# A new order of opening steps, a second two-bank PSUM buffer in blocks 1 and 2, and new turns for side work in a fused attention and two-MLP kernel

## The chip, the cores and the metric

One core of one Trainium2 chip runs the whole program in one launch. The metric is the device time of one execution in microseconds, the median of the runs. Engines are called PE (TensorE), DVE (VectorE), ACT (ScalarE), POOL (GpSimd) and SP (SyncE, which here only issues DMAs).

## The reference

Three stages follow each other; tokens are 8 batches x 576 positions = 4608, the model width is 512.

```python
# 1: attention inside chunks of 64 positions, 8 heads of 64
scores = scale * q_c @ k_c.T;  p = exp(scores - max);  out = (p / (p.sum() + 1e-9)) @ v_c
x = out.transpose(0, 2, 1, 3).reshape(4608, 512)
# 2: gated MLP, w_gate and w_val 512 x 1536, w_out 1536 x 512
xn = x / sqrt(mean(x * x) + 1e-6) * rms_g
g = xn @ w_gate;  y = (g * sigmoid(g) * (xn @ w_val)) @ w_out
# 3: second MLP, w_in 512 x 2048, w_out 2048 x 512, rational activation
h = y @ w_in
P = a0 + a1*h + a2*h*h + a3*h*h*h;  Q = 1 + |b0|*|h| + |b1|*h*h
out = (P / (Q + 1e-6)) @ w_out
```

Everything is float32.

## The kernel before

**Numbers in two parts.** A float32 operand is split into a high part (a cast on ACT) and a low part (value minus high part, usually on DVE), and each product runs as three matmuls, high by high, high by low, low by high (PASSES). Weights arrive as 64-bit words; `words_to_whole` joins the two words of each number: L121 and L126 on ACT, L128 and L131 on DVE. `split` then makes the high part on ACT (L135) and the low part (L137) on DVE, or on POOL where the weight unit's name stands in `ON_POOL`. The low part of an activation tile is made at L390, also on POOL where the tile's name (`x0`, ...) is in `ON_POOL`.

**Tokens.** There are 36 tiles of 128 tokens, four to a block, nine blocks. A tile's attention is a *visit*: `products` (L284) computes on PE into a two-bank PSUM tile `xs` the weighted values of tile x and the scores of tile x+1; DVE normalises (L322) and takes the maximum and subtracts it (L299, L301), ACT takes the exponential p (L308) and the sum of squares (L331), POOL a power (L333, L334), ACT scales xa by it (L475). `transposes` (L351 for p, L354 for xa) writes a second two-bank tile `tp`; ACT copies one half out as pT (L358), DVE multiplies the other by the gain into xf (L383), from which high and low parts go to the block's operand xT (L388, L390) or, in later blocks, to `rawx` and `right`. `xs` and `tp` share one pool tag, "at".

**The first MLP.** Blocks 0 to 2 are *plain*: `cell(j, f)` runs a gate product g and a value product v of 12 matmuls of 512 columns each (L495), with tanh on ACT (L504), L505 and L521 on DVE and a DMA of u to DRAM. A block has 12 cells. Blocks 3 to 8 go in three pairs: `group` computes the same by a scheme with seven products per 2 x 2 blocks (L532, tiles sa and sb, additions L564 and L552 on DVE), whose left operands `combos` and right operands `right_sums` prepare.

**Turns.** After the opening everything is counted in *turns*, a turn being one call of a cell half (12 matmuls) or one step of a group (6 or 12). `plan` maps a turn to side work: `VISIT_AT` is the turn of each visit and `BEHIND` how many turns later its transposes come; `UNIT_AT`, `COMBOS_AT`, `LEFT_AT`, `RIGHT_AT`, `STAGE_AT`, `WO_AT` place weight units, left sums, loads, right sums, staging of the second MLP's weights through DRAM, and the output weights. Blocks 0, 1 and 2 take turns 0 to 23, 24 to 47 and 48 to 71, the pairs turns 72 to 251.

**The output product** of the first MLP starts at turn 252: 90 items of `item_products` (L1039; accumulators a for block 0, then oa and ob). Each item needs a high part (L872) and a low part (L879) of u on ACT and DVE, some need a sum (L864). `left_sums` (L823, L827, L836 on DVE) prepares left operands, `stage` the second MLP's output weights at the turns in `QUAD_AT`. The **second MLP** follows (L1068, L1087).

**Order.** The opening up to the third cell of block 0 is written out by hand: `START` is a string whose letters each advance one generator by a step: 0 to 4 are the first five tiles, a to d the four quarters of weight unit 0, e and f the halves of unit 1, g unit 2, h to j the loads of later units, M, N and O the first three cells, and w one transpose of the identity into an unused bank, which keeps PE occupied. On the engines under `manual_schedule` instructions stay in program order; on the others a scheduler places them, by its own model of waits. All engines are manual in the opening, in plain(0) only SP, in blocks 1 and 2 ACT and DVE, later ACT.

**PSUM.** It has eight banks. `bank` gives single ones (tag "pp"), `two_banks` pairs (tag "at"). `stage_now` picks the counts: 3 singles and 2 pairs in the opening (beside the bank of the idle transposes), 6 and 1 from there to the last group, 4 and 2 in the end.

Of the kernel before, what the change touches and what calls it, by code (L numbers as in the profile page):

```python
# [9 lines left out]
F32 = mybir.dt.float32  # L10
# [13 lines left out]
NPL = 3  # L24
NSTART = 3
START = (
    "120c31wwwwwwwwwwwwwwwwwwwww03020wwww1a0wwwwww20101b4ce020cd21wwwwwww0020wwwwww30gf112131wwww"
    "1c32c0www033c1130132002123aawwwww32www131awww423213024a3wwwwwwwwwwwwww241a2w3bba3b2b343wwwww"
    "wwwMbdec24ddMdMbd4M4eMge4MfeNNdMegfgeiNfNMMgONhfOgfOOggjgNONOgOggg"
)  # L30
ON_POOL = ('w10.0', 'w10.1', 'w10.3', 'w11.0', 'w12.0', 'w12.2', 'x0', 'x1', 'x2', 'x4')
VISIT_AT = (8, 12, 16, 20, 25, 29, 33, 37, 49, 52, 55, 58, 61, 64, 67, 70, 73, 79, 85, 91, 97, 103, 109, 115, 133, 139, 145, 151, 157, 163, 169, 175,)
BEHIND = (4, 4, 4, 4, 4, 4, 4, 4, 2, 2, 2, 2, 2, 2, 2, 2, 4, 4, 4, 4, 4, 4, 4, 4, 4, 4, 4, 4, 4, 4, 4, 4,)
UNIT_AT = (6, 10, 14)
LEFT_AT = (62, 66, 70)
COMBOS_AT = (25, 31, 38, 45, 51, 58)
RIGHT_AT = (73, 120, 180)
STAGE_AT = (28, 74, 102, 134, 152, 171, 194, 222)
STAGE_FROM = (32, 78, 106, 138, 156, 175, 198, 226)
STAGE_EACH = (2, 1, 1, 1, 1, 1, 1, 1)  # L40
WO_AT = (196, 210, 224)
WO_FROM = (204, 218, 232)
OPEN_AT = 246
START_AT = (250, 251)
QUAD_AT = (262, 266, 270, 274, 278, 282, 286, 290, 294, 299, 303, 307, 311, 315, 319, 323)
LEFT_SUMS_AT = (255, 258, 261)
EARLY = 3
BLOCK0 = (
    (-20, "fetch", 0), (-18, "ring", 0), (-17, "split", 0, "B11"), (-16, "split", 0, "B21"), (-15, "sum", 0, "T1"),
# [7 lines left out]
def fused_kernel(  # L57
# [207 lines left out]
    ps_pool = [None]  # L265
    stage_now = [0]

    def bank(name):
        return ps_pool[0].tile([P, W], F32, tag="pp", bufs=(3, 6, 4)[stage_now[0]], name=name)

    def two_banks(shape, name):
        return ps_pool[0].tile(list(shape), F32, tag="at", bufs=(2, 1, 2)[stage_now[0]], name=name)

    def products(x, s):
        ps = two_banks([P, 2, 2, NP, CH], f"xs{x.i if x else ''}_{s.i if s else ''}")
# [62 lines left out]
    def transposes(x, p):  # L338
# [21 lines left out]
        if x:  # L360
# [329 lines left out]
    with ExitStack() as phase:  # L690
# [55 lines left out]

        opening.close()
        ps1 = ExitStack()
        ps_pool[0] = ps1.enter_context(tc.tile_pool(name="ps1", bufs=1, space=PSUM, reuse_waits="tile"))
        stage_now[0] = 1  # L750

        for u in range(3, NG):
            spread(UNIT_AT[u - 3], more[u], 1, 4, 4)
        for n, (turn, behind) in enumerate(zip(VISIT_AT, BEHIND)):
            visit(turn, TB + n, behind)
        spread(RIGHT_AT[0], right_sums(0), 1, 2, 5)
        for t in range(1, NSB):
            spread(RIGHT_AT[t], right_sums(t), 1, 1, 9)
        for g in range(NG):
            spread(COMBOS_AT[g], combos(g), 1, 2, 9)  # L760
        for u in range(3):
            at_turn(LEFT_AT[u], load_left, 0, u)
        for g in range(NF2 // 2):
            steps = stage_left(g)
            at_turn(STAGE_AT[g], next, steps)
            spread(STAGE_FROM[g], steps, 1, STAGE_EACH[g], 24 // STAGE_EACH[g])
        for u in range(3):
            steps = two_halves("wo", u, outs[u])
            at_turn(WO_AT[u], next, steps)
            spread(WO_FROM[u], steps, 1)  # L770

# [14 lines left out]
        with tc.manual_schedule(engines={mybir.EngineType.SP}):  # L786
            plain(0)
        with tc.manual_schedule(engines={mybir.EngineType.Activation, mybir.EngineType.DVE}):
            for j in range(1, NPL):
                plain(j)  # L790
        with tc.manual_schedule(engines={mybir.EngineType.Activation}):
# [146 lines left out]

            at_turn(OPEN_AT, open_o)
            for i in range(2):  # L940
                at_turn(START_AT[i], start_o, i)

            for t in range(NSB):
                running = {}
                used = 0
                for q, k in ORDER:
                    do(TURN[0])
                    if k == 0:
                        running[q] = group(t, q)
# [313 lines left out]
```

## Time and profile before

| | us |
|---|---|
| runs | 1691.86, 1694.39, 1694.63 |
| median | 1694.39 |
| profiled execution, its own time | 1692.62 |
| its span | 1690.8 |
| PE busy | 1665.2 (98% of the span), granted clock 1.00 in every slice |
| DVE busy | 1439.3 (85%) |
| ACT busy | 1058.6 (63%) |
| POOL busy | 346.0 (20%) |

The span is what the profiler saw between first and last instruction; the execution's own time is 1.8 us longer. PE is busy nearly throughout, so what can be gained or lost are the short stretches in which it waits, and they have to be read one by one: in the list of PE's waits, then in the timeline of PE at each of them, then on the engine that PE waited for.

### The profile page before, as it was taken

Reading aid. Unit: us, or ns where it says so; the run is one execution under the profiler, and the core shown is the slowest. Engines: PE = TensorE matmul, PEld = TensorE weight load, DVE = VectorE, ACT = ScalarE, POOL = GpSimd, SP = SyncE. Lnnn points to the kernel's source line nnn. Section 1 sums busy time; section 2 is a strip of 40 time slices with the busy share of each in tenths; the row PEclk is TensorE's granted clock in tenths of the full one; section 3 lists DMA queues with packets and bytes.
Section 4 is the critical chain, followed back from the end, with each engine's and each line's share of the span. In section 5 each row is a group of like instructions: output and inputs, shape, how many; then the busy total and the mean of one; then the engine's idle time right before and its main releaser. Section 6 shows DMA issues by size and latency. Waiting matters only on the chain.

```text
span 1690.8 us, 28465 instructions
## 1 busy us (share of the span) xinstructions
PE 1665.2 (98%) x10981; PEld 1425.3 (84%) x10981; DVE 1439.3 (85%) x1755; ACT 1058.6 (63%) x1592; POOL 346.0 (20%) x293
## 2 busy tenths in 40 slices
PE   8999999999999999999999999999999999999999
PEld 7778877788778887888888899999999999999997
DVE  7868887878779677998897899999999999999986
ACT  7734345555555554466656777777777777777775
POOL 3200000000000000000012343434343434343321
PEclk9999999999999999999999999999999999999999
DMA  8875768777987999287666955555555556555551
GB/s 326 301 237 179 266 238 317 253 272 270 348 319 256 380 350 317 92 300 247 214 212 226 371 202 202 199 201 199 201 197 202 198 202 199 200 199 201 174 194 63
DMA packets 138697, 402.44 MB, mean 238 GB/s; under 512 B 13505, under 2 KB 58561, under 8 KB 124737
## 3 DMA queue, kind: packets, MB, share of 16 engines
q1 hardware_dynamic: 138416, 400.35, 67.3%
q8 instruction: 87, 1.43, 0.3%
q14 instruction: 50, 0.40, 0.1%
q10 hardware_dynamic: 144, 0.26, 0.0%
HBM read 308.29 MB, written 92.27 MB: 237 GB/s over the span
## 4 chain that ended last, share of the span: by engine, by line
PE 79%; DVE 10%; ACT 2%; issue 2%; DMA 1%; POOL 0%; SPq 0%; POOLq 0%; ACTq 0%; DVEq 0%
PE o L1087 23%; PE h L1068 22%; PE sa L532 8%; PE sb L532 6%; PE ob L1039 6%; PE oa L1039 6%; PE g L495 3%; PE v L495 3%; PE xs L284 1%; DMA uring<-ud 1%; DVE u L505 1%; DVE c L564 1%; PE tp L354 1%; DVE u L552 1%; DVE uring L864 1%
## 5 line engine op out<-in xcount | busy, mean ns | idle before, releaser
L1087 PE MATMUL o<-w,ggring 128*128 128x512 f32 x1728 | 418.5, 391 | 0.0
L1068 PEld LDWEIGHTS h<-x2ring,lefts 128*128 128x128 f32 x2982 | 377.3, 191 | 14.2 <-PE h L1068 2.1
L1068 PE MATMUL h<-x2ring,lefts 128*128 128x256 f32 x2982 | 383.1, 283 | 1.0 <-ACT both L1175 0.2
L1087 PEld LDWEIGHTS o<-w,ggring 128*128 128x128 f32 x1728 | 315.2, 188 | 60.7 <-POOL ggring L1164 0.5
L1164 POOL TENSOR_TENSOR ggring<-T,ggring 128x512 fp32r<-128x512 f32 x142 | 181.7, 1302 | 407.1 <-ACT ggring L1163 407.1
L665 POOL TENSOR_TENSOR x2ring<-x2r,x2ring 128x512 fp32r<-128x512 f32 x63 | 116.3, 1851 | 456.2 <-PE oa L1039 362.8
L1143 ACT ACTIVATE work<-h 128x1024 f32<-128x1024 f32 x72 | 73.9, 1026 | 164.5 <-PE h L1068 163.6
L872 ACT CAST rring<-uring 128x1024 fp32r<-128x1024 f32 x90 | 94.2, 1052 | 76.9 <-PE a L1039 23.3
L1180 DVE SCALAR_TENSOR_TENSOR work<-work 128x1024 f32<-128x1024 f32 x72 | 133.9, 1860 | 2.5
L879 DVE TENSOR_TENSOR rring<-uring,rring 128x1024 fp32r<-128x1024 f32 x90 | 111.5, 1243 | 24.4 <-ACT rring L872 20.0
L1145 DVE SCALAR_TENSOR_TENSOR work<-work,small 128x1024 f32<-128x1024 f32 x72 | 92.1, 1280 | 28.2 <-ACT work L1144 28.2
L495 PE MATMUL g<-xT,w 128*128 128x512 f32 (+1 forms) x444 | 108.2, 389 | 2.2 <-POOL w L137 1.3
L532 PE MATMUL sa<-right,left 128*128 128x512 f32 x432 | 109.7, 394 | 0.4 <-DVE u L552 0.4
L495 PE MATMUL v<-xT,w 128*128 128x512 f32 (+1 forms) x444 | 108.8, 389 | 0.0
L532 PE MATMUL sb<-right,left 128*128 128x512 f32 x432 | 108.8, 392 | 0.0
L1181 DVE SCALAR_TENSOR_TENSOR T<-T,small,work 128x1024 f32<-128x1024 f32 x72 | 99.8, 1387 | 2.5
L333 POOL TENSOR_SCALAR ssq<-ssq 128x1 f32<-128x1 f32 x36 | 8.7, 240 | 441.2 <-ACT xf L331 423.9
L495 PEld LDWEIGHTS g<-xT,w 128*128 128x128 f32 x444 | 80.7, 188 | 19.3 <-POOL w L137 1.9
L532 PEld LDWEIGHTS sa<-right,left 128*128 128x128 f32 x432 | 79.9, 188 | 17.5 <-DVE u L552 0.8
L1148 DVE SCALAR_TENSOR_TENSOR T<-T,small,h 128x1024 f32<-128x1024 f32 x72 | 92.2, 1281 | 2.5
L532 PEld LDWEIGHTS sb<-right,left 128*128 128x128 f32 x432 | 80.2, 188 | 16.8 <-DVE u L505 0.2
L495 PEld LDWEIGHTS v<-xT,w 128*128 128x128 f32 x444 | 80.3, 188 | 16.1
(191 smaller groups left out, 2996.6 us busy)
## 6 DMA issues: line engine op xcount, KB each, us to landing
lefts<-wld SPq DMA_DIRECT2D x71, 1536.0 KB, 6.6
left<-wsd SPq DMA_DIRECT2D x30, 2048.0 KB, 9.6
ud<-u SPq DMA_DIRECT2D x108, 256.0 KB, 3.1
uring<-ud SPq DMA_DIRECT2D x54, 512.0 KB, 5.6
raw<-in_w_dram SPq DMA_DIRECT2D x36, 512.0 KB, 5.7
lefts<-wld SPq DMA_DIRECT2D x71, 256.0 KB, 2.7
wsd<-cb SPq DMA_DIRECT2D x48, 256.0 KB, 2.9
raw<-in_w_dram SPq DMA_DIRECT2D x10, 1024.0 KB, 9.8
```

Source lines behind the costliest of these rows:

```text
L495: nc.tensor.matmul(out=acc[:, ts], lhsT=w[:, wh, wk], rhs=x[:, kk, xh, ts], start=kk == 0 and n == 0, stop=kk == KD - 1 and n == 2,)
L532: nc.tensor.matmul(out=acc, lhsT=lhs[:, wh, kk * P:(kk + 1) * P], rhs=rhs[:, kk, xh, :], start=start and kk == 0 and m == 0, stop=kk == 1 ...
L665: nc.gpsimd.tensor_tensor(out=lo, in0=x, in1=hi.bitcast(F32), op=ALU.subtract)
L872: nc.scalar.copy(slot(i)[0], u_of(*items[i]))
L879: nc.vector.tensor_tensor(out=lo, in0=u_of(t, n, f), in1=hi.bitcast(F32), op=ALU.subtract)
L1039: nc.tensor.matmul(**of)
L1068: nc.tensor.matmul(out=out_, lhsT=lhs[:, wh, kk * P:(kk + 1) * P], rhs=rhs[:, kk, xh, :], start=start and kk == 0 and m == 0, stop=kk == 1 ...
L1087: nc.tensor.matmul(out=acc2[j][m], lhsT=ring["gg"][:, p % 2, rh, e * W + m * P:e * W + (m + 1) * P], rhs=ring["quad", f // U][:, wh, f % U ...
L1148: nc.vector.scalar_tensor_tensor(out=T, in0=T, scalar=a1, in1=H, op0=ALU.add, op1=ALU.mult)
L1164: (nc.vector if c == NPAIR - 1 else nc.gpsimd).tensor_tensor(out=r[:, 1, es], in0=Tc[:, es], in1=r[:, 0, es].bitcast(F32), op=ALU.subtract)
L1180: nc.vector.scalar_tensor_tensor(out=V, in0=V, scalar=-2.0, in1=R, op0=ALU.add, op1=ALU.mult)
L1181: nc.vector.scalar_tensor_tensor(out=T, in0=T, scalar=a0, in1=V, op0=ALU.add, op1=ALU.mult)
```

## The change

Seven things are set anew.

1. `START` has 236 letters instead of 250, with 71 idle transposes instead of 85. The first is a run of 10 instead of 21. Tile and weight steps are interleaved in another order, and so are the weights' DMAs.
2. `ON_POOL` keeps two of ten names: `w10.3` (a quarter of weight unit 0) and `x0` (tile 0). The other eight low parts go to DVE.
3. PSUM: blocks 1 and 2 get 4 single banks and 2 pairs. Block 0 and the pairs of blocks keep 6 and 1. A helper `banks_of` closes a pool and opens the next.
4. Visits from the fifth on, and how far their transposes follow, change by a few turns; those of block 2 (turns 49 to 70) do not.
5. `UNIT_AT`, `LEFT_AT`, `COMBOS_AT`, `RIGHT_AT`, `STAGE_AT`, `WO_AT` move by 1 to 8 turns.
6. The first items are prepared at turns 242 and 252 instead of 250 and 251; their buffers are opened at 236 instead of 246.
7. `QUAD_AT` held one tile every 4 or 5 turns from 262 to 323; now tiles come in bunches between 270 and 324. The second of the three left sums starts at turn 254 instead of 258.

Names in the changed file stand five to seven lines lower (L879 there is L885, L823 is L829, L827 is L833).

```diff
 START = (
-    "120c31wwwwwwwwwwwwwwwwwwwww03020wwww1a0wwwwww20101b4ce020cd21wwwwwww0020wwwwww30gf112131wwww"
...
+    "120c23wwwwwwwwww0110wwww20130100c0ca2e024dbwwwwwww01f20wwwwwww310113221g3c00www113www03c1031"
...
-ON_POOL = ('w10.0', 'w10.1', 'w10.3', 'w11.0', 'w12.0', 'w12.2', 'x0', 'x1', 'x2', 'x4')
+ON_POOL = ('w10.3', 'x0')
...
-OPEN_AT = 246
-START_AT = (250, 251)
-QUAD_AT = (262, 266, 270, 274, 278, 282, 286, 290, 294, 299, 303, 307, 311, 315, 319, 323)
-LEFT_SUMS_AT = (255, 258, 261)
+OPEN_AT = 236
+START_AT = (242, 252)
+QUAD_AT = (272, 272, 270, 273, 288, 286, 289, 288, 304, 303, 293, 307, 308, 320, 324, 324)
+LEFT_SUMS_AT = (254, 254, 260)
...
-        return ps_pool[0].tile([P, W], F32, tag="pp", bufs=(3, 6, 4)[stage_now[0]], name=name)
+        return ps_pool[0].tile([P, W], F32, tag="pp", bufs=(3, 4, 6, 4)[stage_now[0]], name=name)
...
-        return ps_pool[0].tile(list(shape), F32, tag="at", bufs=(2, 1, 2)[stage_now[0]], name=name)
+        return ps_pool[0].tile(list(shape), F32, tag="at", bufs=(2, 2, 1, 2)[stage_now[0]], name=name)
...
-        ps_pool[0] = ps1.enter_context(tc.tile_pool(name="ps1", bufs=1, space=PSUM, reuse_waits="tile"))
-        stage_now[0] = 1
+
+        def banks_of(stage):
+            ps1.close()
+            ps_pool[0] = ps1.enter_context(tc.tile_pool(name=f"ps{stage}", bufs=1, space=PSUM, reuse_waits="tile"))
+            stage_now[0] = stage
+
+        banks_of(2)
...
         with tc.manual_schedule(engines={mybir.EngineType.Activation, mybir.EngineType.DVE}):
+            banks_of(1)
             for j in range(1, NPL):
...
+            banks_of(2)
             for t in range(NSB):
```

**First place: PE and DVE around cells 3 to 5 of block 0.** On PE before (g and v are the two products of a cell, the first number after them is the cell; w with a number is a weight unit: 618 is unit 1, 664 unit 2):

```order
L495 MATMUL g_3_714<-xT_363,w_618 128x512 x2
L495 MATMUL v_3_715<-xT_363,w_618 128x512 x2
L284 MATMUL xs_5_755<-v_225,pT_561 64x64 x4
L495 MATMUL g_4_806<-xT_363,w_664 128x512 x12
L495 MATMUL v_4_807<-xT_363,w_664 128x512 x2
L495 MATMUL g_3_714<-xT_363,w_618 128x512 x10
L495 MATMUL v_3_715<-xT_363,w_618 128x512 x10
```

On PE now (604 is unit 1, 662 unit 2):

```order
L495 MATMUL g_3_695<-xT_343,w_604 128x512 x2
L495 MATMUL v_3_696<-xT_343,w_604 128x512 x2
L284 MATMUL xs_5_726<-v_219,pT_543 64x64 x4
L495 MATMUL g_4_777<-xT_343,w_662 128x512 x12
L495 MATMUL v_4_778<-xT_343,w_662 128x512 x12
L495 MATMUL g_5_820<-xT_343,w_662 128x512 x3
L495 MATMUL g_3_695<-xT_343,w_604 128x512 x10
```

The rest of cell 3 stands behind 27 matmuls of cells 4 and 5, where it stood behind 14. It reads the second half of unit 1. On DVE before (raw_231 and w_618 are unit 1, raw_296 unit 2, raw_657 unit 3, raw_624 unit 4):

```order
L521 TENSOR_TENSOR u_2_661<-u_2_661,v_2_644 128x512
L128 TENSOR_SCALAR raw_296<-raw_296 128x1024
L131 ISA raw_296<-raw_296,t 128x1024x2
L137 TENSOR_TENSOR w_618<-raw_231,w_618 128x1024
L128 TENSOR_SCALAR raw_657<-raw_657 128x1024
```

On DVE now (raw_212 and w_604 are unit 1, raw_297 and w_662 unit 2, raw_647 unit 3, raw_619 unit 4):

```order
L521 TENSOR_TENSOR u_2_644<-u_2_644,v_2_627 128x512
L137 TENSOR_TENSOR w_662<-raw_297,w_662 128x1024
L128 TENSOR_SCALAR raw_297<-raw_297 128x1024
L131 ISA raw_297<-raw_297,t 128x1024x2
L128 TENSOR_SCALAR raw_619<-raw_619 128x1024
L128 TENSOR_SCALAR raw_647<-raw_647 128x1024
L137 TENSOR_TENSOR w_662<-raw_297,w_662 128x1024
L137 TENSOR_TENSOR w_604<-raw_212,w_604 128x1024
```

The low part of unit 1's second half stood ahead of unit 3's L128; now it stands behind it and behind unit 2's low part.

**Second place: PE in block 2.** Before, from the transposes of visit 14 to those of visit 15, with what an instruction waits for in brackets:

```order
L354 MATMUL tp_14_2363<-ident,xa_2298 128x128 x3
L495 MATMUL g_3_2389<-xT_1473,w_618 128x512 x12
L495 MATMUL v_3_2390<-xT_1473,w_618 128x512 x4
L284 MATMUL xs_15_2406<-v_2116,pT_2372 64x64 [waits DMAHW1_49,DVE_49]
L284 MATMUL xs_15_2406<-v_2116,pT_2372 64x64 x15
L284 MATMUL xs_15_2406<-k_2241,q_2240 64x64 [waits DMAHW7_49,DMAHW6_49]
L284 MATMUL xs_15_2406<-k_2241,q_2240 64x64 x15
L495 MATMUL v_3_2390<-xT_1473,w_618 128x512 x8
L495 MATMUL g_4_2470<-xT_1473,w_664 128x512 x12
L495 MATMUL v_4_2471<-xT_1473,w_664 128x512
L351 MATMUL tp_15_2487<-ident,p_2446 128x128 [waits PE_49,Activation_49]
```

Now:

```order
L354 MATMUL tp_14_2355<-ident,xa_2306 128x128 x3
L495 MATMUL g_3_2381<-xT_1400,w_604 128x512 x12
L284 MATMUL xs_15_2398<-v_2112,pT_2364 64x64 [waits DMAHW2_49,Activation_49]
L284 MATMUL xs_15_2398<-v_2112,pT_2364 64x64 x15
L284 MATMUL xs_15_2398<-k_2252,q_2251 64x64 [waits DMAHW5_49,DMAHW4_49]
L284 MATMUL xs_15_2398<-k_2252,q_2251 64x64 x15
L495 MATMUL v_3_2382<-xT_1400,w_604 128x512 x12
L495 MATMUL g_4_2462<-xT_1400,w_662 128x512 [waits DVE_49]
L495 MATMUL g_4_2462<-xT_1400,w_662 128x512 x11
L351 MATMUL tp_15_2479<-ident,p_2438 128x128 [waits PE_49,Activation_49]
```

The xs waits for ACT and no longer for DVE; 12 matmuls stand ahead of it where 16 stood, and 24 between it and the next transposes where 21 stood. A cell's first matmul now waits for DVE.

**Third place: DVE at the end of the last group.** Before (the last L552 frees the bank sa_11):

```order
L552 TENSOR_TENSOR u_11_6966<-u_11_6966,c_2_11_6895 128x512
L879 TENSOR_TENSOR rring_6943<-uring_6941,rring_6943 128x2x512
L505 SCALAR_TENSOR_TENSOR u_11_6998<-u_11_6998,sa_10_6807 128x512
L879 TENSOR_TENSOR rring_6943<-uring_6942,rring_6943 128x2x512
L552 TENSOR_TENSOR u_11_6998<-u_11_6998,sa_11_6831 128x512
```

Now:

```order
L552 TENSOR_TENSOR u_11_6960<-u_11_6960,c_2_11_6898 128x512
L552 TENSOR_TENSOR u_9_6774<-u_9_6774,sa_9_6782 128x512
L505 SCALAR_TENSOR_TENSOR u_11_6992<-u_11_6992,sa_10_6808 128x512
L829 TENSOR_TENSOR xo_1_7086<-w_6555 128x1024
L552 TENSOR_TENSOR u_11_6992<-u_11_6992,sa_11_6830 128x512
```

The two low parts of u (L879) between the last L552 are gone from there, and one addition of a left sum (L829) has come in.

## Rows read from the trace of the kernel before

**Rows 1.** PE's waits: instruction, releaser, total us, times, longest us.

```profile
PE tp L351 <- ACT p L308: 3.5, 5, 1.5
PE a L1039 <- DVE u L552: 3.1, 1, 3.1
PE xs L284 <- DVE xf L383: 2.4, 3, 1.4
PE tp L354 <- ACT xa L475: 2.0, 4, 0.8
...
PE oa L1039 <- DVE rring L879: 1.0, 1, 1.0
```

**Rows 2.** Windows in us: length, each engine's busy us, PEclk, DMA share, GB/s.

```profile
112.00:242.00 130.00, 127.04 (x1087) 103.32 (x1086) 108.04 (x188) 54.03 (x102) 6.68 (x18) 1.00 0.60 207
242.00:656.00 414.00, 409.77 (x2940) 332.97 (x2939) 324.30 (x571) 220.23 (x404) 15.08 (x38) 1.00 0.84 304
656.00:662.00 6.00, 2.90 (x13) 1.88 (x12) 6.00 (x9) 3.42 (x4) 0.00 (x0) 1.00 0.97 312
680.00:714.00 34.00, 33.61 (x149) 27.49 (x147) 34.00 (x36) 15.01 (x17) 0.00 (x0) 1.00 0.13 48
720.00:900.00 180.00, 180.00 (x794) 148.62 (x793) 159.84 (x173) 112.46 (x145) 7.57 (x5) 1.00 0.71 242
```

**Rows 3.** Timeline of PE, opening: start us, us, instruction, [idle before <- releaser].

```profile
1.34 4.74 PE L724 MATMUL idle<-ident 128*128 128x128 f32 x21 [1.34 <-POOL ident masks.py:199]
6.01 1.13 PE L284 MATMUL xs<-start 64*64 64x64 f32 x32
...
26.06 0.48 PE L495 MATMUL g<-xT,w 128*128 128x256 f32 x2
```

**Rows 4.** Tile 0's second load: issue by its line (last two numbers, us).

```profile
L438 ACTq DMA_DIRECT2D start<-in_qkv_dram x1: 403/403/403, 0.7 to 0.7; - x1
```

**Rows 5.** DMA issues, first 8 us: count, KB each, us from issue to landing.

```profile
start<-in_qkv_dram ACTq DMA_DIRECT2D x1, 256.0 KB, 3.8
```

**Rows 6.** Low parts of weights by engine: min/median/max ns, first to last start.

```profile
L137 DVE TENSOR_TENSOR w<-raw,w x14: 679/1219/1344, 29.4 to 644.6; 128x1024 fp32r<-128x1024 f32 x13, 128x512 fp32r<-128x512 f32 x1
...
L137 POOL TENSOR_TENSOR w<-raw,w x6: 1307/2037/2582, 25.3 to 52.2; 128x512 fp32r<-128x512 f32 x3, 128x1024 fp32r<-128x1024 f32 x3
```

**Rows 7.** Timeline of DVE, opening and block 0.

```profile
30.18 1.36 DVE L128 TENSOR_SCALAR raw<-raw 128x512 uint32<-128x512 uint32 x1
...
51.18 1.30 DVE L128 TENSOR_SCALAR raw<-raw 128x1024 uint32<-128x1024 uint32 x2
53.22 2.65 DVE L131 CUSTOM_DVE_ANT_0 raw<-raw,t 128x2048 uint16<-128x2048 uint16 x1 [0.75 <-ACT t L126]
```

**Rows 8.** Timeline of POOL, the same stretch.

```profile
29.63 1.63 POOL L137 TENSOR_TENSOR w<-raw,w 128x512 fp32r<-128x512 f32 x1 [1.31 <-ACT w L135]
```

**Rows 9.** Timeline of PE, block 0.

```profile
41.27 2.60 PE L495 MATMUL g<-xT,w 128*128 128x512 f32 x10 [1.13 <-POOL w L137]
...
47.37 0.58 PE L284 MATMUL xs<-v,pT 64*64 64x64 f32 x24 [0.78 <-DVE u L521]
...
71.42 0.66 PE L351 MATMUL tp<-ident,p 128*128 128x128 f32 x4 [1.47 <-ACT p L308]
```

**Rows 10.** Timeline of PE, block 1: two products of a cell.

```profile
143.91 2.90 PE L495 MATMUL g<-xT,w 128*128 128x512 f32 x12
146.65 2.88 PE L495 MATMUL v<-xT,w 128*128 128x512 f32 x12
```

**Rows 11.** Timeline of PE, last group to first item.

```profile
653.66 4.45 PE L532 MATMUL sa<-rightn,left 128*128 128x512 f32 x18
661.21 5.02 PE L1039 MATMUL a<-rring,w 128*128 128x512 f32 x21 [3.10 <-DVE u L552]
```

**Rows 12.** Timeline of DVE, the same stretch.

```profile
657.52 1.22 DVE L879 TENSOR_TENSOR rring<-uring,rring 128x1024 fp32r<-128x1024 f32 x1
...
660.39 0.68 DVE L552 TENSOR_TENSOR u<-u,sa 128x512 f32<-128x512 f32 x1
```

More of the change, by code (lines that the diff above doesn't have):

```diff
@@ L26 @@
 START = (
-    "120c31wwwwwwwwwwwwwwwwwwwww03020wwww1a0wwwwww20101b4ce020cd21wwwwwww0020wwwwww30gf112131wwww"
-    "1c32c0www033c1130132002123aawwwww32www131awww423213024a3wwwwwwwwwwwwww241a2w3bba3b2b343wwwww"
-    "wwwMbdec24ddMdMbd4M4eMge4MfeNNdMegfgeiNfNMMgONhfOgfOOggjgNONOgOggg"
-)
-ON_POOL = ('w10.0', 'w10.1', 'w10.3', 'w11.0', 'w12.0', 'w12.2', 'x0', 'x1', 'x2', 'x4')
[L32 to L39, printed above, removed]
-STAGE_EACH = (2, 1, 1, 1, 1, 1, 1, 1)
-WO_AT = (196, 210, 224)
-WO_FROM = (204, 218, 232)
-OPEN_AT = 246
-START_AT = (250, 251)
-QUAD_AT = (262, 266, 270, 274, 278, 282, 286, 290, 294, 299, 303, 307, 311, 315, 319, 323)
-LEFT_SUMS_AT = (255, 258, 261)
+    "120c23wwwwwwwwww0110wwww20130100c0ca2e024dbwwwwwww01f20wwwwwww310113221g3c00www113www03c1031"
+    "3c213022w3www130wwwww4aa22031a214a42wwwwwwwwwwwwwwwwwww21a3ba23bwwwwwwww3dMb3432b3e2bbedc4wM"
+    "d4MfddedMMNM4egggNeNMei4ffOgfNOMNhOgONMfgggONOggjOgg"
+)
+ON_POOL = ('w10.3', 'x0')
+VISIT_AT = (8, 12, 16, 20, 24, 30, 34, 39, 49, 52, 55, 58, 61, 64, 67, 70, 78, 81, 89, 94, 100, 107, 112, 115, 135, 143, 148, 154, 160, 166, 172, 175)
+BEHIND = (4, 3, 4, 2, 2, 2, 4, 2, 2, 2, 2, 2, 2, 2, 2, 2, 3, 5, 5, 4, 4, 3, 3, 4, 4, 4, 4, 3, 4, 4, 2, 4)
+UNIT_AT = (9, 11, 16)
+LEFT_AT = (60, 67, 68)
+COMBOS_AT = (24, 28, 39, 42, 50, 58)
+RIGHT_AT = (73, 121, 181)
+STAGE_AT = (26, 68, 110, 134, 154, 168, 186, 221)
+STAGE_FROM = (32, 76, 106, 137, 158, 174, 196, 227)
+STAGE_EACH = (2, 1, 1, 1, 1, 1, 1, 1)
+WO_AT = (193, 215, 226)
+WO_FROM = (201, 219, 231)
+OPEN_AT = 236
+START_AT = (242, 252)
+QUAD_AT = (272, 272, 270, 273, 288, 286, 289, 288, 304, 303, 293, 307, 308, 320, 324, 324)
+LEFT_SUMS_AT = (254, 254, 260)
 EARLY = 3
@@ L961, in fused_kernel @@
             ps1.close()
-            ps_pool[0] = ctx.enter_context(tc.tile_pool(name="ps2", bufs=1, space=PSUM, reuse_waits="tile"))
-            stage_now[0] = 2
+            ps_pool[0] = ctx.enter_context(tc.tile_pool(name="ps3", bufs=1, space=PSUM, reuse_waits="tile"))
+            stage_now[0] = 3
             u_ring.append(slab("uring2", (P, 8, W), F32))
```

## Prediction, made before the changed kernel was run

> **What bounds the kernel.** I read the windows first. TensorE (PE) is busy in 127.04 of 130 us in blocks 1 and 2, in 409.77 of 414 in the groups and in all of the 180 us from 720 on, at a granted clock of 1.00 throughout [rows 2]. No change of order can shorten its matmuls, so I read the list of its waits next [rows 1], then its timeline at each wait, then the engine that it waited for. The waits fall into five places: the opening (the first product of cell 0 starts at 26.06 us [rows 3]), block 0, the visits of blocks 1 and 2, the passage from the last group to the output product, and one at about 714. In all of these PE waits for a chain of DVE, ACT or POOL work. Each part of the change aims at one of them, and what it is worth is how much of that wait goes, less any wait that it makes.
>
> **Part 1, opening.** PE starts with 21 idle transposes that end at 1.34 + 4.74 = 6.08, and tile 0's scores start right then [rows 3]. The later of tile 0's two loads is issued at 0.7 and takes 3.8 to land [rows 4, 5], so it is there at 4.5. Ten transposes at the mean of 4.74/21 = 0.23 us end at 3.6. The scores are then bound by the load and start at 4.6, 1.4 us earlier, and the whole chain behind them (DVE, ACT, transposes) is shifted with it.
>
> Eight low parts go from POOL to DVE: five of 512 columns and three of 1024, at 0.68 and 1.22 us [rows 6], 5 x 0.68 + 3 x 1.22 = 7.1 us more DVE work. What comes back is that DVE runs slowly beside POOL: the 512-wide L128 at 30.18 took 1.36 us where two 1024-wide ones took 1.30 together, and L131 at 53.22 took 2.65 [rows 7]. Seven instructions up to 53.22 are stretched in this way; I put the sum at 8 us, an estimate from these two (0.7 and 1.4 us lost) and wider ones between them. So I count DVE's load as unchanged. Each moved low part itself is ready sooner (a half unit 1.22 instead of up to 2.58 [rows 6]).
>
> The Trainium skill's "SBUF — State Buffer" (Who interferes with whom) says that GpSimd and a DVE instruction that needs both ports, or has two SBUF inputs, hold a pair of ports in turn, and that the second to issue stands still until the first is done. The rows agree: POOL's low part of 29.63 lasted 1.63, to 31.26 [rows 8], and 30.18's L128 ended 0.28 after, at 31.54 [rows 7]. By that rule all 8 us come back, and the two low parts left on POOL can still stop DVE twice; by shared speed rather than a lock less would come back. I keep the 8.
>
> With the first scores 1.4 earlier, and cell 0's weights and tiles no longer made by POOL, I get cell 0 starting 1.4 earlier, and cell 2, which waited 1.13 for a low part of unit 1 on POOL until 41.27 [rows 9], about 2.9 earlier: its 2.5 on POOL become 1.2 on DVE. The next visit's products, at 47.37 after 0.78 of waiting for L521, follow cell 2 directly and come at 44.2, 3.2 earlier, with that wait kept.
>
> Then a new wait. In the changed order, 12 + 12 + 3 matmuls of cells 4 and 5 follow, then cell 3's rest, which needs the low part of unit 1's second half. Twelve matmuls of 512 columns take 2.72 to 2.74 (143.91 to 146.65 [rows 10]), 0.227 each; with 4 matmuls of cell 3 and the xs work (0.8) PE gets there at 44.2 + 0.8 + 31 x 0.227 = 52.0. On DVE that low part now stands behind an L128 of unit 3. Unit 3's first L128 started at about 51.2 before [rows 7], held by its load and by ACT, neither of which the change clearly speeds up. After it come 0.65 for L128 and two low parts at 1.13 (starts of neighbours): ready at 51.2 + 0.65 + 2.26 = 54.1. PE waits 2.1 us, in a place where it did not wait before. Of the 3.2 gained, 1.1 is left at the end of block 0's first half. The transposes at 71.42 waited 1.47 for p [rows 9]; their DVE queue is as full as before, so I leave that wait alone.
> Bounds: 3.5 gained if unit 3 lands early enough, 2 lost if a load interleaved with it delays it by another 3. Value: -1.0.
>
> **Part 2, block 0 into block 1.** The xs of visit 8 to 9 waited 1.4 us for DVE's L383, the longest of three such waits that add up to 2.4 [rows 1]. Now two pairs are there from block 1 on, so this xs waits for the banks of the pool before it. I expect about 0.4 left. Value: -1.0, between -1.4 and +0.5.
>
> **Part 3, blocks 1 and 2.** PE idles 130 - 127.0 = 3.0 us there [rows 2]. The two other waits for L383 (2.4 - 1.4 = 1.0) go: with a second pair the xs waits for pT alone, and ACT has 12 matmuls (2.7 us) for it. The rest, 2.0, are the transposes that wait for p and xa. Where 21 matmuls stood between xs and the transposes, 24 stand now, 0.7 us more for the same chain (the turns in block 2 are the same), and the longest single wait of each kind is 1.5 and 0.8 us in the whole run [rows 1], most of those here about half a microsecond. The price is two banks fewer for cells: a cell waits for L505 and L521 of the cell two before, 36 matmuls or 8.2 us back, and these take 0.7 us and their queue. DVE is busy 108 of 130 us [rows 2], so its queue is seldom longer than a few us, and I count nothing. Value: -1.0 - 1.6 = -2.6; from -3.0 (all waits gone) to +2 (a few cells late).
>
> **Part 4, turns of the groups.** PE idles 4.2 us of 414 [rows 2], in some ten small waits behind DVE or ACT. Moved turns remove some and make others: 0, between -2 and +2.
>
> **Part 5, groups into items.** PE finished the last group at about 653.66 + 4.45 = 658.1 and stood until 661.21 [rows 11], because the first accumulator needs the bank that the last L552 reads, and that started at 660.39 behind low parts L879, the first at 657.52 [rows 12]; DVE was busy 6.00 of 6 us there [rows 2]. Two L879 (1.14 each between neighbours) are taken from in front of it and one left sum (1.14) put there, 1.1 less; and the first product of the changed order has three matmuls (0.7) before the bank is needed. Value: -1.1 - 0.7 = -1.8, between -3.1 and 0.
>
> **Part 6, staging.** PE waited 1.0 for L879 [rows 1] at the end of a stretch in which DVE was busy 34.00 of 34 us [rows 2]. The staging of weights now starts 8 turns later, so about 10 us of DVE work leave the stretch before: the wait goes. The bunches fall into 720 to 900, where DVE was busy 159.8 of 180 and PE never idle [rows 2], 20 us of room. Value: -1.0, between -1.1 and +2.
>
> **Sum.** -1.0 - 1.0 - 2.6 + 0 - 1.8 - 1.0 = -7.4 us. The profiled execution took 1692.6, its span 1690.8; so 1685.2 for one like it. The median lies 1.8 higher, at 1694.4, and the runs spread over 2.8; 1694.4 - 7.4 = 1687.0. I take 1686.5, nearer the median's figure. That is 0.47% faster; 0.2%, or 3.4 us, is about what can be told from no change here.
>
> **Rivals.**
> (a) *The opening gives back more.* Unit 3's load is late by 3 us or DVE's queue between 50 and 72 is longer, so the wait in block 0 is 5 us and not 2; then part 1 is +2 and, with parts 2 and 3 at half, the sum is 2 - 0.5 - 1.3 - 2.8 = -2.6: 1691.5, no change that can be told. For it: the 7.1 us of low parts come on top of DVE's queue if the stretch beside POOL is not wholly given back. Against it: ACT, which feeds it, has the same work.
> (b) *All waits named go, and the load order helps.* Part 1 keeps its 3.2, parts 2, 3, 5 and 6 take all: -3.2 - 1.4 - 3.0 - 3.1 - 1.0 = -11.7: 1682.5. For it: every one of these waits is for a chain that the change shortens. Against it: the order of DVE shows a new wait outright.
> (c) *Slower: four banks are too few.* In blocks 1 and 2, DVE runs in program order with the visits' steps in front of L505 and L521. If a visit's chain delays them past 8.2 us, each of the 24 cells there loses about the 0.6 us of one DVE instruction: +14 and the sum +14 - 7.4 + 2.6 = +9: 1703.5. It decides from 0.34 us a cell on (24 x 0.34 = 8.2, and with the other parts at -4.8 that is +3.4). For it: the changed order shows a DVE wait at the cell's first matmul. Against it: 22 us of DVE room in 130.
> (d) *The clock.* With 14 idle transposes fewer and a new wait, PE is empty longer in the opening. The wait of 3.1 us at 658 left the granted clock at 1.00 [rows 2]; a longer one is not in this trace. If the clock fell to its lower level for some 4 us, 2 us would be lost. The Trainium skill's "TensorE: Matmul & The Clock Gate" (Part 1) says that an idle stretch takes the clock from 2.4 to 1.2 GHz; no run here shows it. This adds to (a) and is no case of its own.
>
> **Chances.** Forecast 0.50; (b) 0.17; (a) 0.21; (c) 0.12. Slower holds (c) but for its mild end, 0.10; same takes (a) and a little of the rest, 0.20; faster 0.70. The range from 1680 to 1694 leaves out the larger half of (c) and the far ends of (a) and (b). Around the forecast alone it is 1683 to 1690.
>
> **What would show it.** Right: the first scores at 4.6; a wait of about 2 us before cell 3's third matmul near 52, released by L137; no xs waiting for L383 in blocks 1 and 2; PE's stop at the first item 1 to 1.5 us instead of 3.1; none near 710. Wrong: PE waits at cells' first matmuls for L505 or L521 in blocks 1 and 2; PE waits between 720 and 900; a granted clock below 1; the first product of cell 0 not before 25.5.

## The result

The changed kernel took 1678.47 us (median of 5 runs, 1675.92 to 1678.90), the kernel before 1692.54 beside it (1691.35 to 1694.63). The ratio is 0.9911, 95% interval 0.9897 to 0.9926: 15 us faster by the ratio, twice the 7.4 us forecast, and outside the stated range. The profiled execution took 1678.9 us with a span of 1677.1.

**PE's waits** in the changed kernel (instruction, releaser, total us, times, longest us); they answer to [rows 1]:

```profile
PE xs L284 <- DMA k<-in_qkv_dram: 2.0, 3, 1.3
PE xs L284 <- issue: 1.9, 2, 1.1
PE xs L284 <- DVE u L521: 1.7, 1, 1.7
PE tp L351 <- ACT p L308: 1.4, 2, 0.8
...
PE a L1046 <- DVE u L552: 1.1, 1, 1.1
...
PE ob L1046 <- DVE rring L885: 0.9, 2, 0.5
```

The waits of xs for L383 are gone, those of transposes for xa too, those for p are down from 3.5 to 1.4, and the one at the first item from 3.1 to 1.1. The waits for loads of k are up from 0.7 us to 2.0, that for L521 from 0.8 to 1.7 and those for instructions ("issue") from 1.1 to 1.9; two for L885 are new.

**Windows** of the changed kernel (columns as in [rows 2]; 646 is where its items start):

```profile
112.00:272.00 160.00, 160.00 (x1396) 131.92 (x1396) 132.29 (x233) 69.64 (x131) 8.30 (x23) 1.00 0.70 242
272.00:646.00 374.00, 372.31 (x2601) 305.33 (x2600) 300.05 (x525) 206.24 (x375) 12.63 (x32) 1.00 0.85 309
646.00:720.00 74.00, 72.90 (x322) 59.99 (x321) 62.76 (x63) 33.90 (x39) 0.00 (x0) 1.00 0.57 200
720.00:895.00 175.00, 174.07 (x764) 142.44 (x763) 159.07 (x170) 106.90 (x141) 11.73 (x7) 1.00 0.67 226
```

PE is never idle from 112 to 272, and 1.7 us in the groups, where it idled 4.2 of 414 [rows 2]; between 720 and 895 it now idles 0.9, where it did not before.

**Where the time went, stage by stage.** For this I follow PE's matmuls in order, give each its back-to-back spacing (0.227 us for 512 columns, half for 256, the small ones by their own), and compare the two traces at equal amounts of work done. How much earlier the changed kernel is, and what each stage adds:

| up to (us in the trace of before) | earlier by | of the stage | forecast |
|---|---|---|---|
| end of block 0 (105) | 0.3 | 0.3 | 1.0 |
| into block 1 (112) | 1.9 | 1.5 | 1.0 |
| end of block 2 (272) | 6.2 | 4.4 | 2.6 |
| end of the groups (657) | 11.9 | 5.7 | 0 |
| items running (664) | 13.9 | 2.0 | 1.8 |
| after the wait at 714 (730) | 15.5 | 1.6 | 1.0 |
| items (840) | 13.0 | -2.5 | in the 1.0 |
| last matmul (1687) | 13.7 | 0.7 | 0 |

The largest miss is the groups' 5.7 us, which I had put at nothing. The sum is 13.7 us between two single executions; the 15 us are from five runs of each.

### The profile page after: what moved, and what is told of

It is laid out like the page before. It is cut to its first block, busy times and chain, and to the rows that moved or that the text cites. A ratio compares the mean times of both kernels' runs of the same rounds, so it can differ in the third digit from the quotient of the medians.

```text
span 1677.1 us, 28374 instructions
## 1 busy us (share of the span) xinstructions
PE 1659.8 (99%) x10967; PEld 1425.3 (85%) x10967; DVE 1438.2 (86%) x1763; ACT 1057.2 (63%) x1592; POOL 329.8 (20%) x285
## 4 chain that ended last, share of the span: by engine, by line
PE 88%; DVE 3%; DMA 2%; issue 1%; ACT 1%; POOL 0%; SPq 0%; DVEq 0%; ACTq 0%
PE o L1094 24%; PE h L1075 22%; PE sa L532 10%; PE sb L532 8%; PE oa L1046 5%; PE ob L1046 5%; PE v L495 5%; PE g L495 5%; PE a L1046 2%; PE xs L284 2%; DVE rring L885 1%; PE tp L351 1%; PE tp L354 1%; PE ob L1054 0%; PE oa L1054 0%
## 5 line engine op out<-in xcount | busy, mean ns | idle before, releaser
L1075 PEld LDWEIGHTS h<-x2ring,lefts 128*128 128x128 f32 x2982 | 377.2, 191 | 13.9 <-PE h L1075 2.1
L885 DVE TENSOR_TENSOR rring<-uring,rring 128x1024 fp32r<-128x1024 f32 x90 | 112.4, 1255 | 21.7 <-ACT rring L878 21.5
```

Source lines behind the costliest of these rows:

```text
L885: nc.vector.tensor_tensor(out=lo, in0=u_of(t, n, f), in1=hi.bitcast(F32), op=ALU.subtract)
L1075: nc.tensor.matmul(out=out_, lhsT=lhs[:, wh, kk * P:(kk + 1) * P], rhs=rhs[:, kk, xh, :], start=start and kk == 0 and m == 0, stop=kk == 1 ...
```

## The experiments

All ran against the kernel before on the same chip, 5 rounds; the changed kernel stands at 0.9911 of it, measured apart from them. Every ratio here has an interval of about 0.0014 to either side (2.4 us) unless it is written out. A difference to the changed kernel is one of two such ratios, known to some 0.0019 or 3.2 us: of the parts put back, only the group turns, their visits and the early turns are slower by more than that. What is smaller is read from the traces, at equal work as in the table above. One thousandth is 1.7 us. "Table" means a line of the numbers at the head of the kernel.

**Group turns put back.** In the changed kernel the last 16 entries of `VISIT_AT` and `BEHIND`, and `RIGHT_AT`, `STAGE_AT`, `STAGE_FROM`, `WO_AT`, `WO_FROM` as before:

```diff
-RIGHT_AT = (73, 121, 181)
-STAGE_AT = (26, 68, 110, 134, 154, 168, 186, 221)
+RIGHT_AT = (73, 120, 180)
+STAGE_AT = (28, 74, 102, 134, 152, 171, 194, 222)
...
-WO_AT = (193, 215, 226)
+WO_AT = (196, 210, 224)
```

> The changed kernel with the old turns of visits, their transposes, right sums, staging and output weights in the groups (turns 72 to 251); all else as changed. Theory (the moved turns took the waits of transposes and group products away): the waits for p, xa, u and c come back, some 4 to 6 us, and the kernel is at about 1683.5. Rival (the prediction's: these turns are worth nothing, the gain in the groups follows from what came before them): within 2 us of the changed kernel, 1678.5.

Measured 0.9943 (0.9930 to 0.9955), median 1685.20: 0.0032 or 5.4 us slower than the changed kernel. PE's waits in its groups:

```profile
PE tp L354 <- ACT xa L475: 1.0, 2, 0.8
PE tp L351 <- ACT p L308: 0.8, 1, 0.8
PE sa L532 <- ACT rightt L421: 0.5, 1, 0.5
PE sa L532 <- DVE u L552: 0.4, 1, 0.4
```

These came back with the turns, in the changed kernel with all else new; by the trace its groups gain 1.2 us on the kernel before instead of 5.7. The theory holds; the forecast's nothing does not.

What the turns do shows at one visit. PE before, and the same visit in the changed kernel:

```profile
430.52 0.65 PE L284 MATMUL xs<-k,q 64*64 64x64 f32 x32
431.10 1.66 PE L532 MATMUL sb<-right,left 128*128 128x512 f32 x6
432.59 2.88 PE L532 MATMUL sa<-right,left 128*128 128x512 f32 x12
436.29 0.66 PE L351 MATMUL tp<-ident,p 128*128 128x128 f32 x4 [0.81 <-ACT p L308]
```

```profile
426.88 1.66 PE L532 MATMUL sa<-right,left 128*128 128x512 f32 x6
428.38 4.25 PE L532 MATMUL sa<-rightn,left 128*128 128x512 f32 x18
432.47 0.60 PE L351 MATMUL tp<-ident,p 128*128 128x128 f32 x4
```

From the matmuls behind xs (431.10, now 426.88) to the end of p on ACT (436.24, now 431.48) it took 5.1 us before and 4.6 now. The 18 matmuls between gave 4.4 us of room, the 24 give 5.6. The three visits of the groups whose transposes waited in the kernel before had 12, 18 and 18 matmuls there; now they have 48, 24 and 38, and with the group turns put back 12, 18 and 18 again. `BEHIND` counts turns, and a turn of a group is 6 or 12 matmuls, so the same number means different room. Room is not all: two visits of the changed kernel have 13 and do not wait, so the other work on DVE and ACT at the place counts as well.

**All group turns alone**, in the kernel before (the same tables, the other way round):

> The kernel before with all new turns of the groups (visits, right sums, staging, output weights) as its only edits. Theory (the group turns are worth 5.5 us by themselves): 4.5 to 6 us faster than before, about 1688. Rival (they need what comes before or after): under 3 us.

Measured 0.9968 (0.9956 to 0.9979): 5.4 us faster. The groups' part of the gain needs nothing of the rest. By the trace its groups gain 5.2 us, of which 1.9 are lost again at the first item, where the granted clock falls (last section). The trace has no wait of the groups' own work left, only two for k:

```profile
PE a L1039 <- DVE u L552: 2.8, 1, 2.8
PE xs L284 <- DMA k<-in_qkv_dram: 2.3, 2, 2.0
```

**Visits of the groups alone**, in the kernel before, and **visits put back** or **staging put back** in the changed kernel:

```diff
-VISIT_AT = (8, 12, 16, 20, 24, 30, 34, 39, 49, 52, 55, 58, 61, 64, 67, 70, 78, 81, 89, 94, 100, 107, 112, 115, 135, 143, 148, 154, 160, 166, 172, 175)
-BEHIND = (4, 3, 4, 2, 2, 2, 4, 2, 2, 2, 2, 2, 2, 2, 2, 2, 3, 5, 5, 4, 4, 3, 3, 4, 4, 4, 4, 3, 4, 4, 2, 4)
+VISIT_AT = (8, 12, 16, 20, 24, 30, 34, 39, 49, 52, 55, 58, 61, 64, 67, 70, 73, 79, 85, 91, 97, 103, 109, 115, 133, 139, 145, 151, 157, 163, 169, 175)
+BEHIND = (4, 3, 4, 2, 2, 2, 4, 2, 2, 2, 2, 2, 2, 2, 2, 2, 4, 4, 4, 4, 4, 4, 4, 4, 4, 4, 4, 4, 4, 4, 4, 4)
```

> The kernel before with the new turns of the groups' visits as its only edit. Theory (the visits' turns alone take the transposes' waits for p and xa away): 3 to 5 us faster than before, about 1690, with the waits at 315 and 435 us gone. Rival (visits and staging fit each other and only move together): within 1.5 us of before or slower, as the old visits with the new staging were 3 us worse than all old turns.

> The changed kernel with the old turns of the visits in the groups alone. Theory (p and xa were late at these turns): most of the 5.5 us that all group turns are worth comes back, 1682 to 1684, with waits of transposes near 310 and 430 us. Rival (staging and output weights, which load DVE and ACT, set it): under 1.5 us.

> The changed kernel with the old turns of staging and output weights in the groups alone. Theory (visits set it): within 1.5 us of the changed kernel. Rival (staging sets it): 3 to 5 us slower, with group products waiting for u, c or right parts.

Measured: the visits alone 0.9983 (0.9974 to 0.9992), 2.9 us faster. Visits put back 0.9962, 8.6 us slower than the changed kernel, more than the whole set put back. Staging put back 0.9907, no difference that can be told. So the turns of the visits carry the groups' gain, in the kernel before by about half alone (3.4 us of its groups by the trace); how the rest divides among staging and right sums was not separated. The old visits among the new staging pay more than they did before, and this trace shows for what. On SP's queue (start us, us, issue):

```profile
441.74 0.39 SPq L615 DMA_DIRECT2D left<-wsd  x1
442.22 0.40 SPq L447 DMA_DIRECT2D q<-in_qkv_dram  x1
442.72 0.38 SPq L448 DMA_DIRECT2D k<-in_qkv_dram  x1
```

and on PE:

```profile
452.71 1.13 PE L284 MATMUL xs<-k,q 64*64 64x64 f32 x32 [3.05 <-DMA k<-in_qkv_dram]
```

The visit's loads were issued right behind a load of left operands (2 MB), and k, issued at 442.72, landed 9.9 us later, where its median is 4.4 us in the changed kernel; PE waited for it until 452.71. Two such waits make 4.3 us there, and behind this one the granted clock is 0.50 (453 to 455), so that the next six matmuls took 2.61 us instead of some 1.6.

**One pair of banks**, in the changed kernel, and **the pair alone**, in the kernel before:

```diff
-        return ps_pool[0].tile([P, W], F32, tag="pp", bufs=(3, 4, 6, 4)[stage_now[0]], name=name)
+        return ps_pool[0].tile([P, W], F32, tag="pp", bufs=(3, 6, 6, 4)[stage_now[0]], name=name)
...
-        return ps_pool[0].tile(list(shape), F32, tag="at", bufs=(2, 2, 1, 2)[stage_now[0]], name=name)
+        return ps_pool[0].tile(list(shape), F32, tag="at", bufs=(2, 1, 1, 2)[stage_now[0]], name=name)
```

> The changed kernel with 6 single banks and 1 pair in blocks 1 and 2. Theory (the second pair takes all waits of blocks 1 and 2 away): 4 to 5 us slower than the changed kernel, about 1683, with xs waiting for L383 and transposes for p and xa between 112 and 260 us. The prediction's size: 2.6 to 3.6 slower, 1681.6. Rival (the new place of the visits in block 1 does it): within 1 us.

> The kernel before with the second pair of banks in blocks 1 and 2 as its only edit. Theory (the pair takes the waits of blocks 1 and 2 away, and in the kernel without it the new turns did the same, so each is enough): 2.5 to 4.5 us faster than before, about 1690, no wait between 112 and 260 us. Rival (only the new turns do it): within 1 us of before, the transposes still wait for p and xa near 206, 217, 228 and 239 us.

Measured: without the second pair 0.9916, 0.8 us slower and within the uncertainty; its trace has no wait in blocks 1 and 2 but one for instructions (0.8 us, at block 1's start, which the changed kernel has as well), and at equal work the two blocks gain 4.5 us with one pair, as much as with two. The pair alone gave 0.9987 (0.9978 to 0.9995), 2.2 us by the times; its trace between 112 and 272 us:

```profile
PE tp L347 <- ACT p L304: 1.2, 2, 0.7
PE tp L350 <- ACT xa L471: 0.8, 2, 0.4
```

The xs no longer wait for L383 (1.0 us of block 1), but the transposes wait as they did. At the passage into block 1 the wait of 1.4 us for L383 is gone too, and others of 0.9, 0.7 and 0.6 us have come in its place; by its trace the passage and the two blocks gain 0.2 us together, so the 2.2 by the times are not explained there. My theory, that each of pair and turns is enough, is half wrong: the turns are enough, the pair is not.

**Early turns put back**, in the changed kernel: visits of blocks 0 to 2 (those of block 2 are the same), `UNIT_AT`, `LEFT_AT`, `COMBOS_AT`. **Left sums put back**: `COMBOS_AT` alone. **Left sums alone**, in the kernel before:

```diff
-COMBOS_AT = (24, 28, 39, 42, 50, 58)
+COMBOS_AT = (25, 31, 38, 45, 51, 58)
```

> The changed kernel with the old turns of the visits of blocks 0 to 2, of weight units, left loads and left sums. Theory (the pair alone is enough): within 1.5 us of the changed kernel, at 1679 to 1680. Rival (only the new turns do it): 4 to 6 us slower, about 1684, with waits of transposes in block 2.

> The changed kernel with the old turns of the left sums (COMBOS_AT) alone. Theory (the left sum of weight unit 4, one turn later, puts its DVE work in front of the visits' in block 2, and nothing else of blocks 1 and 2 matters): 3 to 3.5 us slower than the changed kernel, about 1682, transposes wait for p and xa near 200, 211, 223 and 234 us. Rival (the visits' turns in block 1 and the rest): under 1 us.

> The kernel before with the new turns of the left sums as its only edit. Theory: 2.5 to 3.5 us faster than before, about 1690.5, no transposes waiting in block 2. Rival (the second pair is needed as well): within 1 us of before.

Measured: early turns put back 0.9938, 4.6 us slower, as the rival had it; left sums put back 0.9926, 2.5 us slower, less than the times can tell; left sums alone 0.9987 (0.9977 to 0.9997), 2.2 us faster than before. Left sums put back, PE between 112 and 272:

```profile
PE tp L354 <- ACT xa L475: 0.9, 2, 0.4
PE tp L351 <- ACT p L308: 0.7, 1, 0.7
```

Left sums alone, the same stretch:

```profile
PE xs L284 <- DVE xf L383: 1.4, 2, 0.7
```

The two lists are complements. The left sums' turn takes the transposes' waits of block 2 away, with one pair of banks or two; the pair takes the xs waits of block 1 away, and the other new turns do so without it (one pair in the changed kernel has none). DVE shows how the left sums act, before and with them alone:

```profile
230.26 1.28 DVE L220 TENSOR_TENSOR sums<-w 128x512 f32<-128x512 f32 x2
...
232.06 0.68 DVE L383 TENSOR_TENSOR rawx<-tp,small 128x512 f32<-128x512 f32 x1
```

```profile
225.11 1.29 DVE L220 TENSOR_TENSOR sums<-w 128x512 f32<-128x512 f32 x2
...
227.50 0.69 DVE L383 TENSOR_TENSOR rawx<-tp,small 128x512 f32<-128x512 f32 x1 [0.51 <-ACT pT L358]
```

Before, additions of the left sum hold L383 until 2.4 us after the transposes that it reads, and every later step of the visits on DVE with it; moved, they are done in time and L383 waits for ACT alone. Which of the five left sums that moved matters was not tried apart. The rest of the early turns (visits, their transposes, weight units, left loads, not separated) is worth some 2 us at the passage into block 1, where the trace with them put back has waits of 0.9, 0.7 and 0.6 us that the changed kernel has not.

**Opening put back**, in the changed kernel (`START` and `ON_POOL` as before):

> The changed kernel with the old opening steps and the old list of parts on GpSimd. Theory (the new opening is worth little, because a stretch of 3.4 us at half clock takes back what the earlier start gives): within 1.5 us of the changed kernel, 1678 to 1680, and the granted clock stays at full. Rival (the prediction's: 1 us and, with all of its gain kept, 3.2): 1 to 3 us slower, 1679.5 to 1681.5.

Measured 0.9918, median 1681.42: 1.2 us slower by the ratio, and in the one trace of it the last matmul ends within 0.1 us of the changed kernel's. The new opening is worth nothing that one can tell. The other traces say the same: against the trace of the kernel before, block 0 ends between 1.3 us earlier and 0.5 later in five more traces with the old opening, and between 2.1 earlier and 1.5 later in the nine with the new one (the changed kernel's among them).

**Even staging turns.** `QUAD_AT` as before, in the changed kernel; and the same with the last quarter of weight unit 0 split on DVE (`ON_POOL = ('x0',)`):

> The changed kernel with the old even turns of staging the second MLP's output weights. Theory (the bunches make PE wait for L885 at 737, 741 and 796 us, about 1.5 to 2.5 us, and take 1 us at 714 away): within 1.5 us of the changed kernel to either side, the waits behind 730 gone and one near 700 back. Rival (the prediction's: the later start is worth 1 us and the bunches cost nothing): 1 us slower, 1679.5.

> The changed kernel with the old even turns of staging, and with the last quarter of weight unit 0 split on DVE, so that only tile 0 is left on GpSimd. Theory (that low part on GpSimd holds a store in SP's queue, behind it unit 4's load, behind that ACT's tanh of cell 2, and so the visit's products at 47 us): the xs at 47 us starts 1 to 2 us earlier, and the kernel is 0.5 to 1.5 us faster than with the old staging turns alone (0.9897 of before), at about 1675.5, the fastest here. Rival (the time is given back at 52 us, where cell 3 waits for unit 1's low part, as the prediction had it): the xs is earlier, the time the same as with the old staging turns alone.

Measured 0.9897 (0.9884 to 0.9911), median 1676.74, and 0.9898 (0.9883 to 0.9913), median 1677.84. The first is the fastest kernel here; by its times it can't be told from the changed one (0.9911), but its trace says which part is gone. From 640 on PE waits there only at the first item and once in the second MLP:

```profile
PE a L1046 <- DVE u L552: 1.1, 1, 1.1
PE h L1075 <- ACT both L1135: 0.5, 1, 0.5
```

The bunches had cost two waits for L885, and no wait near 700 came back with the even turns. So staging that early does not make that wait. At equal work between 730 and 840, all nine traces with the bunches lose 1.7 to 3.3 us against the kernel before, the two with even turns nothing: the bunches cost time, though the times alone cannot tell it. In the second kernel the xs of the visit waits only 0.78 us for L521 and starts at 46.50 instead of 47.14, but cell 3 then waits, and at 71 us the two are level:

```profile
46.50 0.68 PE L284 MATMUL xs<-v,pT 64*64 64x64 f32 x26 [0.78 <-DVE u L521]
...
55.47 2.57 PE L495 MATMUL g<-xT,w 128*128 128x512 f32 x10 [0.30 <-DVE w L137]
...
70.69 0.66 PE L351 MATMUL tp<-ident,p 128*128 128x128 f32 x4 [0.92 <-ACT p L308]
```

The xs came 0.6 us earlier, not 1 to 2. The rival of that run was right: the time is given back.

**Start of the items put back**, in the changed kernel:

```diff
-OPEN_AT = 236
-START_AT = (242, 252)
+OPEN_AT = 246
+START_AT = (250, 251)
...
-LEFT_SUMS_AT = (254, 254, 260)
+LEFT_SUMS_AT = (255, 258, 261)
```

> The changed kernel with the old turns of the first items, their buffers and the output weights' left sums. Theory: the wait at the first item is 3 us again instead of 1.1, and the one of 1.1 us at 700 for L885 returns although staging still starts late: 2 to 3 us slower, about 1681.5. The prediction (the later staging alone took the second wait away): 1.8 us slower, no wait near 700.

Measured 0.9926, 2.5 us slower, 2.3 by the trace between 657 and 730. PE, timeline:

```profile
648.49 3.68 PE L1046 MATMUL a<-rring,w 128*128 128x512 f32 x15 [1.60 <-DVE u L552]
...
700.90 3.28 PE L1046 MATMUL oa<-rring,so 128*128 128x512 f32 x13 [0.68 <-DVE rring L885]
```

The wait at the first item is 1.6 + 0.2 (its first low part) instead of 1.1, less than the 3 I expected, and the one near 700 is back although the staging still starts late. The items' start and the output weights' left sums, moved together here, took it away.

## Why the prediction was wrong

**The step that failed is part 4, the turns of the groups:** "Moved turns remove some and make others: 0, between -2 and +2." It measured -5.7 in the trace, -5.4 by putting it back and -5.4 alone. I had read 4.2 us of PE idle there [rows 2] and called the moves a wash without following one. They are not: the transposes waited for p and xa at three visits that had 12 to 18 matmuls of room, and the new turns give those three 24 to 48, without making as much elsewhere. With 5.5 in that place the sum is 12.9 and the forecast 1681. The list of waits held only part of the answer. Its idle went from 4.2 to 1.7 us; counted by how late the matmuls behind these waits start, that is 5.3 to 2.3. The other 2.7 us of the stage are delays too short for the list, or spread over many matmuls; they were not followed.

**Part 1, opening:** size near (0.3 against 1.0), by luck: the same opening put block 0's end anywhere from 1.5 us later to 2.1 earlier in other traces, and the path was wrong. The first scores did start at 4.64, but cell 0 at 26.79 and not 1.4 earlier than 26.06 [rows 3]. I had the new wait at 52 us; it came at 47, at the visit's products. On POOL, then ACT, then PE of the changed kernel:

```profile
35.23 1.33 POOL L137 TENSOR_TENSOR w<-raw,w 128x512 fp32r<-128x512 f32 x1 [13.43 <-ACT w L135]
```

```profile
43.86 1.11 ACT L121 ACTIVATE raw<-raw 128x1024 f32<-128x1024 f32 x1 [3.99 <-DMA raw<-in_w_dram]
44.88 0.58 ACT L504 ACTIVATE u<-g 128x512 f32<-128x512 f32 x1
```

```profile
47.14 0.58 PE L284 MATMUL xs<-v,pT 64*64 64x64 f32 x24 [1.72 <-DVE u L521]
```

The last quarter left on POOL ends at 36.56; a store of it stands in SP's queue ahead of unit 4's load, which is issued at 37.50; ACT's L121 waits for that load, and the tanh of cell 2 stands behind it, then L505, L521 and xs. With that quarter on DVE the load goes out at 36.62, and the tanh then stands ahead of L121, so that run does not tell the two apart. I had followed DVE's order at this place but neither SP's nor ACT's. DVE did get lighter: it was busy 40.58 us of the stretch 26 to 72, against 42.63 before, though most of the moved low parts lie there, and a 512-wide L128 at 31.75 took 0.42 us where the one of 30.18 had taken 1.36 [rows 7]. What the Trainium skill's "SBUF — State Buffer" (Who interferes with whom) says of the pair of ports, that the second of the two engines stands still, agrees with both.

**Part 2** came out at 1.5 instead of 1.0, by the early turns and not by the pair: with one pair that passage is as short, with the early turns put back it is 2 us longer.

**Part 3** came out at 4.4 instead of 2.6. Its waits did all go, but of my two reasons the pair explains at most 1.0 us, and "24 matmuls instead of 21" nothing: the pair alone gives 24 in the same place and its transposes still wait. DVE's load from the left sums was the cause of the transposes' waits. The price that I feared, four single banks, did not come: no cell waited.

**Part 5** was right in size and path: 2.0 against 1.8. With the items' start put back, half of it goes (1.0 is left). PE's first item, three matmuls, then the last L552:

```profile
646.03 0.84 PE L1046 MATMUL a<-rring,w 128*128 128x512 f32 x3
647.98 4.40 PE L1046 MATMUL a<-rring,w 128*128 128x512 f32 x18 [1.10 <-DVE u L552]
```

**Part 6** had the wrong sign for staging. The wait at 714 went by the start of the items and the left sums, and the bunches, which I had given 20 us of DVE room in 180, made waits of 0.42 and 0.46 at L885 and cost 2.5 us by the trace between 730 and 840. Room over a long stretch says nothing of four tiles that come within four turns.

**Rivals.** (b) was nearest: 11.7 of 13.7 us, but by the wrong parts. (c) did not come. (a) did not either: the opening's new wait was 1.7 us in this trace, though 3.5 in another of the same opening. The clock of (d) did fall, in most traces of the new opening at that wait (last section). Three of the signs named for being wrong came: a granted clock below 1, cell 0's first product later than 25.5, and waits between 720 and 900.

## What to carry to other kernels

A table of turns that moves many small pieces is not worth zero because pieces move both ways: list the waits in the stretch, and for each count the work that stands between a chain's start and its use before and now, and ask which pieces meet there. Follow every queue at a place, not only the one of the engine that waits: here, by the trace, a low part on GpSimd reached TensorE through SP's queue, a load and ACT's order. And put one part back at a time: two of the parts that looked like the cause (the pair of banks, the late staging) were not. Where one trace shows a gain of 1 us, look at the same place in other traces with the same part.

## What the runs showed of the hardware

The clock fell in the opening of the profiled execution. Windows of the changed kernel (us, PE busy, PEclk, DMA share, GB/s):

```profile
20.00:22.00 2.00, 0.95 (x14) 0.98 1.01 406
22.00:24.00 2.00, 2.00 (x11) 0.50 1.03 412
24.00:26.00 2.00, 2.00 (x15) 0.67 1.03 406
```

PE had waited 0.54 us for k and 1.07 us for instructions, with small matmuls between, and then ran its 19 idle transposes at 1.2 GHz:

```profile
21.32 3.80 PE L724 MATMUL idle<-ident 128*128 128x128 f32 x19
```

In the trace with one pair, which has the same opening, the same 19 took 2.29 us and cell 0 started 1.2 us earlier. The Trainium skill's "TensorE: Matmul & The Clock Gate" (Part 1) says that idling takes the clock from 2.4 to 1.2 GHz, and here the trace shows it, after these two short pauses.

That delay was swallowed by the xs at 47 us, which waits for the load of unit 4 either way. But PE then stands longer there, and the clock can fall at that place instead. With one pair it does (PE, then a window):

```profile
47.84 0.92 PE L284 MATMUL xs<-v,pT 64*64 64x64 f32 x24 [3.45 <-DVE u L521]
51.12 4.45 PE L495 MATMUL g<-xT,w 128*128 128x512 f32 x12
```

```profile
48.00:50.00 2.00, 2.00 (x27) 0.50 1.02 406
```

The 12 matmuls of cell 4 took 4.45 us, where the changed kernel's took 3.04. Of the nine traces with the new opening, seven waited 1.9 to 3.5 us at this xs and had the clock at 0.50 behind it; the two others, with 1.7 and 2.2 us, kept it. In the six with the old opening this wait is 0.78 us and the clock stays there (it fell in one of them at 22 us, that of the pair alone). This is one reason why the earlier start of the new opening is worth nothing.

Nor does the wait of 3.1 us at the first item always leave the clock at 1.00, as it did in the one trace that the prediction had [rows 2, 11]. With the left sums alone, in the kernel before:

```profile
657.83 0.77 PE L1039 MATMUL a<-rring,w 128*128 128x512 f32 x1 [3.10 <-DVE u L552]
```

```profile
658.00:660.00 2.00, 2.00 (x5) 0.50 0.96 301
```

With the groups' visits alone it is the same after 3.10 us, with all group turns alone after 2.84 and with the pair alone after 1.60; between 657 and 664 the first three lose 1.4 to 1.9 us against the trace of the kernel before. None of the traces with the new start of the items, where the wait is near 1.1 us, has it. So the change takes away more there, in such executions, than the 2.0 us of the table.

The spread of the runs goes with the clock as well. Of the 55 runs of the kernel before that stood beside the experiments, the three with a mean granted clock of 1.000 took 1691.2 us on average, the 31 at 0.999 1693.5, the 14 at 0.998 1695.1, the four at 0.997 1695.0 and the three at 0.996 1697.1.

Also new to me: a load of 0.25 MB that is issued right behind one of 2 MB on the same queue took 9.9 us where 4.4 is the median; the large one took 9.1.
